# Attention products in single precision on pairs of 64x64 tiles instead of three half-precision products each

## The chip, the cores and the metric

One Trainium2 chip; the kernel runs on one of its eight cores. The metric is device time of one launch in microseconds (us), less is better. The kernel before takes 2324.98 us (median of 3 runs, 2323.55 to 2327.02).

## The reference, cut to what matters

Three stages follow each other on 4 x 768 = 3072 tokens: a linear attention with a delta rule (8 heads of 48), a mixture of 8 experts weighted by a Sinkhorn-normalized gate, and a gated two-layer network.

```python
def _attn_ref(q, k, v, beta):               # (4, 8, 768, 48)
    k_n = k / (np.linalg.norm(k, axis=-1, keepdims=True) + 1e-06)
    for t in range(S):
        y[:, :, t] = einsum('bhd,bhde->bhe', q[:, :, t], state)
        v_old = einsum('bhde,bhd->bhe', state, k_n[:, :, t])
        state = state + beta_t * outer(k_n[:, :, t], v_t - v_old)
def _moe_ref(x, w_gate, w1, w2):            # x (3072, 384), 8 experts, 1024 wide
    P = exp(x @ w_gate - max)
    for _ in range(8): normalize rows of P, then columns, times N / E
    for e in range(E): out += P[:, e:e+1] * (maximum(x @ w1[e], 0) @ w2[e])
def _moe2_ref(x, w1, w2, w3, w_out):
    return ((x @ w1) * (x @ w2) @ w3) @ w_out
```

## The kernel before

The attention is computed in 12 chunks of 64 tokens. The 32 heads (batch times head) lie as 16 groups of two: one head of a group on partitions 0 to 63, the other on 64 to 127. A matmul for both is a pair, one on the upper left 64x64 corner of the array and one on the lower right (`tile_position`). A chunk's work is done in two halves (hf) of 8 groups, so that a half's product fills one PSUM bank: 8 pairs.

Within a chunk the recurrence is solved with a triangular matrix T per head. The names that the rows below use:

- `gram`: k times k transposed, from `kt` (keys transposed). Its lower blocks go to `a0` (printed as `a`) and `g12` (printed as `g`).
- `invert(j)`: for the two chunks of pair j together, VectorE inverts 32x32 unit triangular blocks: a transposition into `asys` (L590), the product with beta (`bm`), recursive doubling with products and reductions, and two transpositions back (L650 into `asys`, L652 into `a0`). It is one long chain on DVE.
- `tt_make`: from the inverted blocks, two small fp32 products of 32x32 tiles (`xm` reads `asys` and `g12`; `om` reads `g12` and the staging tile `stg`), then T times beta as `tt`.
- `prep_q`: q and k give `pt`, masked.
- `seq(c)`, the chain over the chunks: `ks` (state times k, subtracted from `vs`, giving r), `um` (T times r gives u), `um2` (k times u added onto the state in PSUM, copied to s), `ym` (q times s plus pt times u, the output).

All these products except `xm` and `om` are made in half precision without losing single precision: every operand is split into a high and a low fp16 part, and `three` (L569) issues three matmul pairs for each. So each operand costs a copy to fp16 on ACT (the high part) and a subtraction on DVE or POOL (the low part), and the scales that keep the parts in range: k is divided by its norm and multiplied by 1024 before the split (`prep_k`), q by a power of two found from its largest sum of squares (`scale_chain`), v by one found in a first pass over all of v (`vscan`), T by 256. `kt` comes from PE transposes of the fp16 keys with an identity.

After a chunk its output goes to DRAM and back (`xs_d`, a change of layout), and the gate's logits (`lg`) and expert 0 (`e0`, fp32r matmuls of 128x128 by 256 columns, tiles `xr`, `wA`, `hA`) are computed for it; e0 of chunks 10 and 11 is left for later. When the logits of chunk 11 are there, the Sinkhorn iterations run and the remaining experts and the last network follow (phases B and C: 128x512 and 128x256 matmuls).

What sets the order: nothing is ordered by hand. `Plan.order` takes each operation with its engines, planned duration, priority and the buffers (`Ring`) it needs, and fixes an order for every engine. The constants of the plan (`PAIR`, the planned duration of one pair) only move instructions; the chip runs each engine's list in that order and waits where data or a buffer are late. Buffers that matter here: three for `kt` and k, one for v, two for `a0`, one for `asys`, `t`, `prod` and `g12`; attention has three PSUM banks at a time. SP issues nearly all transfers, in order.

Of the kernel before, what the change touches and what calls it, by code (L numbers as in the profile page):

```python
# [6 lines left out]
F32 = mybir.dt.float32  # L7
# [17 lines left out]
KS = 1024.0  # L25
TS = 256.0
KSL = 3
K16 = 3
NKR = 3
NA0 = 2  # L30
NSU = 2
NST = 2
NV = 1
# [4 lines left out]
NQ = 2  # L38
# [7 lines left out]
PAIR = .036  # L46
ZDVE = (0,)
ZPOOL = (1,)
# [240 lines left out]
def act(n, psum=False):  # L289
    return (n / 1.2 + (55 if psum else 95)) / 1000  # L290
# [14 lines left out]
class Kernel:  # L305
# [56 lines left out]
    def setup(self):  # L362
# [41 lines left out]
        id0 = lambda: T["a0"][:, NA0 - 1, 0:4].rearrange("p s c -> p (s c)")  # L404
        self.dma(id0, lambda: a["ident"], 65536, [], ["id0"], -10)
        for i in range(K16):
            dst = lambda i=i: T["k16"][:, i]
            prio = (-9, -8, 8, 8)[i]
            if i in ZDVE:
                g.op({"DVE": 2048 / 1900 + .07}, lambda e, dst=dst: nc.vector.memset(dst(), 0.0), w=[("kz", i)], prio=prio)  # L410
            elif i in ZPOOL:
                g.op({"POOL": 2048 / 1200 + .07}, lambda e, dst=dst: nc.gpsimd.memset(dst(), 0.0), w=[("kz", i)], prio=prio)
            else:
                self.dma(lambda dst=dst: dst().rearrange(FLAT), lambda: a["zeros"][:, 0:2048], 256 * 2048, [], [("kz", i)], prio)
        for nm in ("u16", "s16"):
# [6 lines left out]
        self.kring = Ring(range(KSL), fifo=True)  # L422
        self.k16ring = Ring(range(K16), fifo=True)
        self.sring = Ring(range(NSU), fifo=True)
        self.uring = Ring(range(NSU), fifo=True)
        self.stg = Ring(range(NST))
        self.kraw = Ring(range(NKR), fifo=True)
        self.tt16ring = Ring(range(NTC), fifo=True)
        self.qraw = Ring([0], fifo=True)
        self.vring = Ring(range(NV), fifo=True)  # L430
        self.qring = Ring(range(NQ), fifo=True)
        self.ptring = Ring(range(NPT), fifo=True)
# [7 lines left out]
        self.K, self.K16, self.S, self.Q, self.PT, self.TT, self.X, self.a0 = {}, {}, {}, {}, {}, {}, {}, {}  # L440
        self.SX = None


    def sc(self, i):
        return self.T["sml"][:, i:i + 1]

    def scale_chain(self, src, dst, inv, bits, prio, key):

        nc, g = self.nc, self.g
        s = self.psum.new("attn")  # L450
        c = self.sc
        g.op({"PE": .11}, lambda e: self.mm(self.ps(s, 1), self.T["ones"], c(src), start=True, stop=True),
             r=["ones", ("sml", src)], w=[s], prio=prio)

        def chain(e):
            nc.vector.tensor_scalar(out=c(src), in0=self.ps(s, 1), scalar1=1e-30, scalar2=None, op0=ALU.max)
        g.op({"DVE": .1}, chain, r=[s], w=[("sml", src)], prio=prio)
        g.op({"ACT": .15}, lambda e: nc.scalar.activation(out=c(src), in_=c(src), func=AF.Sqrt), r=[], w=[("sml", src)],
             prio=prio)

        def fin(e):
            nc.vector.tensor_scalar(out=c(src).bitcast(I32), in0=c(src).bitcast(I32), scalar1=0x7F800000, scalar2=None,
                                    op0=ALU.bitwise_and)
            nc.vector.tensor_scalar(out=c(inv), in0=c(src), scalar1=2.0 ** -bits, scalar2=None, op0=ALU.mult)
            nc.vector.reciprocal(out=c(dst), in_=c(inv))
        g.op({"DVE": .3}, fin, r=[], w=[("sml", src), ("sml", inv), ("sml", dst)], prio=prio)
# [4 lines left out]
    def vscan(self):  # L471

        nc, g, T = self.nc, self.g, self.T
        for i in range(NCH):
            s = (self.yring, self.vring)[i % 2].new()
            v = (lambda s=s: T["vs"][:, s.at].rearrange("p g d -> p (g d)")) if i % 2 else (
                lambda s=s: T["xst"][:, s.at].rearrange("p h f -> p (h f)")[:, 0:768])
            self.dma(v, lambda i=i: self.vsrc(i), 393216, [], [s], -3)
            g.op({"ACT": act(768) + .09}, lambda e, v=v, i=i: nc.scalar.activation(
                out=v(), in_=v(), func=AF.Square, accum_out=self.sc(41 + i)), w=[s, ("sml", 41 + i)], prio=VP)  # L480
        g.op({"DVE": .1}, lambda e: nc.vector.tensor_reduce(out=self.sc(12), in_=T["sml"][:, 41:41 + NCH], axis=AX.X, op=ALU.add),
             r=[("sml", i) for i in range(41, 41 + NCH)], w=[("sml", 12)], prio=-1)
        self.scale_chain(12, 13, 14, 10, -1, "v")


    def prep_k(self, c):
        nc, g, T = self.nc, self.g, self.T
        pr = 10.0 * (c // 2)
        pe = lambda d: d if c < 2 else {"POOL": d["POOL"]}
        kr = self.kraw.new()  # L490
        raw = [kr]
        kraw = lambda: T["kraw"][:, kr.at]
        self.dma(lambda: kraw().rearrange("p g d -> p (g d)"), lambda: self.a["k"][c], 393216, [], raw, pr - 20 + c % 2)
        pb = self.pring.new()
        sq = lambda: T["prod"][:, pb.at, 0:768].rearrange("p (g d) -> p g d", d=D)
        g.op(pe({"POOL": pool2(768), "DVE": dve(768)}), lambda e: self.tt(e, sq(), kraw(), kraw(), ALU.mult),
             r=raw, w=[pb, "sq"], prio=pr)
        nr = lambda i: T["nrm"][:, i]
        g.op({"DVE": dve(768)}, lambda e: nc.vector.tensor_reduce(out=nr(0), in_=sq(), axis=AX.X, op=ALU.add),
# [27 lines left out]
        if c % 2 == 0:  # L527
            self.a0[c // 2] = self.aring.new()
# [911 lines left out]
```

## Time and profile before

| | us |
|---|---|
| median of 3 runs | 2324.98 |
| profiled execution, its own time | 2326.66 |
| its span, first to last instruction | 2324.9 |
| PE busy in the span | 2191.2 (94%) |
| DVE busy | 1325.7 (57%) |
| ACT busy | 696.5 (30%) |
| POOL busy | 335.2 (14%) |
| mean granted TensorE clock | 0.959 |

The page is read by stage: the shares above are averages over the attention (about the first 550 us) and the experts and the last network after it, which have different limits. PE's busy time is modelled, so a busy PE need not be PE at its best: the granted clock beside it says which of its two levels it had. An fp32 matmul of the program shows as two MATMUL records with a weight load each; an fp16 one as one of each. Idle time of an engine is followed by what ended it.

### The profile page before, as it was taken

How to read it: one execution, taken by the hardware profiler on the slowest of the kernel's cores; microseconds unless marked ns; L12 is line 12 of the kernel's file. 1: busy time of each engine (PE TensorE's matmuls, PEld its weight loads, DVE VectorE, ACT ScalarE, POOL GpSimd, SP SyncE). 2: the span in 40 equal slices, each digit the busy share in tenths (PEclk: the TensorE clock that was granted, in tenths of full speed). 3: DMA queues.
4: the chain of work that ended last, by engine and by line, in shares of the span. 5: the costliest groups of instructions: out<-in, count | busy, mean ns of one | idle time of the engine just before them, and what ended most of it. 6: DMA issues, size and time to landing. Idle time of an engine off the chain costs nothing.

```text
span 2324.9 us, 47410 instructions
## 1 busy us (share of the span) xinstructions
PE 2191.2 (94%) x20519; PEld 1926.3 (83%) x20519; DVE 1325.7 (57%) x2312; ACT 696.5 (30%) x1398; POOL 335.2 (14%) x324
## 2 busy tenths in 40 slices
PE   2589999997799999999999999999999999999999
PEld 2488888887688888888888888888888888999999
DVE  8787787674877777777644444444444444322332
ACT  6446546544222223232211211111111111233332
POOL 5323334113211101111000000000000001300000
PEclk6697898898999999999999999999999999999999
DMA  6212112114533233232210101101010034500000
GB/s 196 64 52 76 53 52 63 51 41 125 169 94 111 94 95 116 87 118 90 79 46 14 46 14 46 41 19 46 14 46 28 19 122 104 109 15 21 15 15 21
DMA packets 135009, 152.60 MB, mean 66 GB/s; under 512 B 10640, under 2 KB 105168, under 8 KB 134032
## 3 DMA queue, kind: packets, MB, share of 16 engines
q1 hardware_dynamic: 115920, 127.82, 17.8%
q0 software_dynamic: 18880, 21.76, 3.7%
q8 instruction: 160, 2.62, 0.5%
q14 instruction: 49, 0.40, 0.1%
HBM read 118.24 MB, written 31.29 MB: 64 GB/s over the span
## 4 chain that ended last, share of the span: by engine, by line
PE 74%; DVE 2%; issue 1%; DMA 0%; ACT 0%; POOL 0%; SPq 0%; DVEq 0%; ACTq 0%; POOLq 0%
PE b L327 74%; DVE acc L338 1%; DVE p L341 0%; DVE p L338 0%; DMA xst<-xs_d 0%; DMA rawB<-in_moe_w 0%; DMA xs_d<-xst 0%; DVE cs L995 0%; DVE xT L338 0%; DVE rs L991 0%; DVE tmp L338 0%; DVE rs L992 0%; DVE cv L1205 0%; DVE hA L341 0%; DVE cv L341 0%
## 5 line engine op out<-in xcount | busy, mean ns | idle before, releaser
L327 PE MATMUL b<-xT,wA 128*128 128x512 f32 x2520 | 584.7, 389 | 0.0
L327 PEld LDWEIGHTS b<-xT,wA 128*128 128x128 f32 x2520 | 473.0, 188 | 98.2
L327 PE MATMUL b<-hA,wA 128*128 128x512 f32 (+1 forms) x2322 | 499.1, 356 | 3.9 <-DVE hA L341 3.1
L327 PEld LDWEIGHTS b<-hA,wA 128*128 128x128 f32 x2322 | 389.0, 191 | 65.9 <-DVE hA L341 4.8
L327 PE MATMUL b<-hB,wA 128*128 128x512 f32 (+1 forms) x1566 | 406.1, 387 | 0.0
L327 PEld LDWEIGHTS b<-hB,wA 128*128 128x128 f32 x1566 | 292.0, 189 | 58.9
L338 DVE TENSOR_TENSOR tmp<-b,pb 128x512 f32<-128x512 f32 x252 | 174.0, 691 | 241.3 <-PE b L327 240.7
L1108 ACT ACTIVATE hA<-b 128x512 fp32r<-128x512 f32 (+1 forms) x178 | 104.2, 585 | 649.9 <-PE b L327 639.8
L341 DVE SCALAR_TENSOR_TENSOR hA<-b,hA 128x512 fp32r<-128x512 f32 (+1 forms) x218 | 147.4, 677 | 178.4 <-ACT hA L1108 169.7
L327 PE MATMUL b<-xr,wA 128*128 128x256 f32 (+1 forms) x1368 | 238.7, 327 | 2.6 <-ACT wA L331 2.2
L327 PEld LDWEIGHTS b<-xr,wA 128*128 128x128 f32 x1368 | 204.6, 193 | 24.1 <-ACT wA L331 2.6
L327 PE MATMUL b<-xr,xT 128*128 128x256 f32 x1728 | 209.9, 283 | 0.0
L327 PEld LDWEIGHTS b<-xr,xT 128*128 128x128 f32 x1728 | 209.3, 192 | 0.0
L341 DVE SCALAR_TENSOR_TENSOR hB<-b,hB 128x512 fp32r<-128x512 f32 (+1 forms) x174 | 118.3, 681 | 152.2 <-ACT hB L1108 152.2
L338 DVE TENSOR_TENSOR acc<-acc,tmp 128x512 f32<-128x512 f32 x250 | 181.4, 726 | 6.5
L1108 ACT ACTIVATE hB<-b 128x512 fp32r<-128x512 f32 (+1 forms) x174 | 102.3, 588 | 196.4 <-PE b L327 196.4
L338 DVE TENSOR_TENSOR cv<-b,cv 128x256 f32<-128x256 f32 x96 | 40.7, 424 | 162.2 <-PE b L327 161.6
L338 POOL TENSOR_TENSOR wA<-rawB,wA 128x768 fp32r<-128x768 f32 x17 | 33.0, 1939 | 674.7 <-ACT wA L331 674.7
L338 POOL TENSOR_TENSOR cv<-cv 128x256 f32<-128x256 f32 (+1 forms) x68 | 52.6, 774 | 300.9 <-DVE cv L1205 174.6
L327 PEld LDWEIGHTS <-kt 64*64 64x64 f16 x3360 | 71.1, 123 | 21.3 <-issue 16.9
L331 ACT ACTIVATE cvs<-cv 128x256 fp32r<-128x256 f32 x72 | 28.9, 402 | 165.0 <-DVE cv L341 165.0
L331 ACT ACTIVATE wA<-rawB 128x768 fp32r<-128x768 f32 x56 | 45.9, 842 | 73.5 <-PE b L327 39.0
(174 smaller groups left out, 2222.4 us busy)
## 6 DMA issues: line engine op xcount, KB each, us to landing
pb<-p_d SPq DMA_DIRECT2D x90, 256.0 KB, 3.2
rawB<-in_moe_w SPq DMA_DIRECT2D x112, 192.0 KB, 3.3
w_d<-cvs SPq DMA_DIRECT2D x112, 128.0 KB, 2.0
cvr<-in_w3T SPq DMA_DIRECT2D x32, 256.0 KB, 2.6
xT<-w_d POOLq DMA_DIRECT2D x32, 256.0 KB, 3.5
vs<-in_v SPq DMA_DIRECT2D x18, 384.0 KB, 3.9
qraw<-in_qT SPq DMA_DIRECT2D x12, 512.0 KB, 4.2
cvr<-in_moe_w SPq DMA_DIRECT2D x24, 256.0 KB, 2.6
```

The costliest lines, as they stand in the source:

```text
L327: self.nc.tensor.matmul(*args, skip_group_check=True, **kw)
L331: self.nc.scalar.activation(out=out, in_=in_, func=AF.Copy, **({} if scale is None else {"scale": scale}))
L338: self.E[eng].tensor_tensor(out=out, in0=in0, in1=in1, op=op)
L341: self.nc.vector.scalar_tensor_tensor(out=out, in0=in0, scalar=scalar, in1=in1, op0=op0, op1=op1)
L1108: g.op({"ACT": act(N, True)}, lambda e, s=s, h=h, hx=hx, N=N: nc.scalar.activation(out=self.hv(h, hx, N)[:, 0], in_=self.ps(s, N), func=AF ...
```

## The change

The fp16 parts, the scales and the transposes go. Every attention product is issued as one fp32 matmul pair (`pair`) where `three` issued three fp16 pairs. k stays as it was loaded; its transposed form is loaded from DRAM (`kT`, laid out on the host). The norms of k are found for both chunks of a pair at once and folded in elsewhere: beta is divided by the norm twice, v is multiplied by the norm before T is applied. q and v are not scaled. The mask of `pt` is multiplied in by DVE straight from PSUM. The planned duration of a pair becomes .118; rings become four for k and kt, three for v and q. What follows `e0` (phases B and C) is not touched.

```diff
-PAIR = .036
+PAIR = .118
@@ prep_k
-        g.op(pe({"POOL": pool2(768), "DVE": dve(768)}), lambda e: self.tt(e, sq(), kraw(), kraw(), ALU.mult),
+        self.dma(lambda: T["kt"][:, k.at].rearrange("p g t -> p (g t)"), lambda: self.a["kT"][c], 524288, [], [k], pr - 20.1 + c % 2)
+        g.op({"ACT": act(768)}, lambda e: nc.scalar.activation(out=sq(), in_=T["kraw"][:, kr.at], func=AF.Square), r=[kr], w=[pb], prio=pr)
...
+                v.tensor_scalar(out=nv(), in0=nr(1), scalar1=0.5, scalar2=1e-6, op0=ALU.mult, op1=ALU.add)
+                v.reciprocal(out=nr(2), in_=nv())
+                v.tensor_tensor(out=bm(), in0=bm(), in1=nr(2), op=ALU.mult)
+                v.tensor_tensor(out=bm(), in0=bm(), in1=nr(2), op=ALU.mult)
...
-            for i in range(2):
-                def tr(e, i=i, hf=hf, s=s):
-                            self.mm(o[r, y], T["k16"][r, kc.at, hf, i, y], T["i128"][r, r], start=True, stop=True, tile_position=(64 * p, 64 * p))
-                     lambda e, i=i, hf=hf, s=s: self.copy(e, T["kt"][:, k.at, hf, i], self.ps(s, 8, 64)),
...
-                    self.three(lambda r: o[r, y], kt(0, y), kt(1, y), kt(0, y), kt(1, y))
+                    self.pair(lambda r: o[r, y], kt, kt, rows=D)
@@
-    def three(self, o, lh, ll, rh, rl, first=True, last=True):
-        for l, r, st, sp in ((lh, rh, first, False), (lh, rl, False, False), (ll, rh, False, last)):
-            for p in range(2):
-                rows = slice(64 * p, 64 * p + 64)
-                self.mm(o(rows), l(rows), r(rows), start=st, stop=sp, tile_position=(64 * p, 64 * p))
+    def pair(self, o, l, r, rows=64, cols=64, start=True, stop=True):
+        for p in range(2):
+            k = slice(64 * p, 64 * p + rows)
+            self.mm(o(slice(64 * p, 64 * p + cols)), l(k), r(k), start=start, stop=stop, tile_position=(64 * p, 64 * p))
@@ prep_q (the scaling, the split and the staging of q go)
+            g.op({"DVE": dve(512)}, lambda e, s=s, pt=pt, hf=hf: self.tt(
+                e, T["pt"][:, pt.at // 2, pt.at % 2], self.ps(s, 8, 64),
+                T["masks"][:, 0:64].rearrange("p (o t) -> p o t", o=1).to_broadcast([128, 8, 64]), ALU.mult), r=[s, "masks"], w=[pt], prio=pr)
@@ seq
-        g.op({"ACT": act(768) + .09}, lambda e: self.copy(e, va(), va(), self.sc(13)), r=[("sml", 13)], w=vk, prio=pr)
+        g.op({"POOL": 1.5, "DVE": dve(768) + .08}, lambda e: self.tt(
+            e, va(), va(), T["nv"][:, 16 * c:16 * c + 16].rearrange("p (s o) -> p s o", o=1).to_broadcast([128, NG, D]), ALU.mult),
+            r=[("nv", j)], w=vk, prio=10.0 * j + .5)
...
-            g.op({"ACT": act(384)}, lambda e, vv=vv, hf=hf: self.copy("ACT", T["r16"][:, 0, hf], vv()),
-            g.op({"DVE": dve(384), "POOL": pool2(384)}, lambda e, vv=vv, hf=hf: self.tt(
-                e, T["r16"][:, 1, hf], vv(), T["r16"][:, 0, hf], ALU.subtract),
...
-            g.op({"ACT": act(384, True)}, lambda e, s=s, hf=hf: self.copy(
-                "ACT", part("u16", u, hf, 0), self.ps(s, 8, D), 1.0 / TS), r=[s, "u16z"], w=uk[:1], prio=pr)
-            g.op({"DVE": dve(384)}, lambda e, s=s, hf=hf: self.stt(
-                part("u16", u, hf, 1), self.ps(s, 8, D), 1.0 / TS, part("u16", u, hf, 0), ALU.mult, ALU.subtract),
+            g.op({"ACT": act(384, True)}, lambda e, s=s, gs=gs: self.copy("ACT", T["u"][:, u.at, gs], self.ps(s, 8, D)),
+                 r=[s], w=[(u, hf)], prio=pr)
```

How the lists of DVE move, at two places in the fourth of the six rounds (pair 3). The number behind a name is the buffer; `b` is a PSUM bank, `a` is a0.

DVE right behind the inversion's last transposition, before:

```order
L652 STREAM_TRANSPOSE a_109<-t 128x32x32
L338 TENSOR_TENSOR stg<-a_109,bm 128x8x32
L338 TENSOR_TENSOR stg<-b_131,bm 32x8x32 x2
L338 TENSOR_TENSOR tt_94<-stg,tt_94 128x512
L338 TENSOR_TENSOR stg<-b_134,bm 32x8x32 x2
L341 SCALAR_TENSOR_TENSOR a_109<-b_128,masks,a_109 128x256
L338 TENSOR_TENSOR tt_94<-stg,tt_94 128x512
L338 TENSOR_TENSOR stg<-a_109,bm 128x8x32
L341 SCALAR_TENSOR_TENSOR a_109<-b_129,masks,a_109 128x256
L341 SCALAR_TENSOR_TENSOR u_98<-b_132,u_98 128x384
L341 SCALAR_TENSOR_TENSOR u_98<-b_133,u_98 128x384
```

The same place on DVE now:

```order
L561 STREAM_TRANSPOSE a_107<-t 128x32x32
L332 TENSOR_TENSOR tt<-a_107,bm 128x8x32 x3
L332 TENSOR_TENSOR tt<-b_131,bm 32x8x32 x2
L335 SCALAR_TENSOR_TENSOR a_107<-b_126,masks,a_107 128x256
L332 TENSOR_TENSOR tt<-b_129,bm 32x8x32 x2
L335 SCALAR_TENSOR_TENSOR vs<-b_127,vs 128x384
L332 TENSOR_TENSOR vs<-vs,nv 128x768
L335 SCALAR_TENSOR_TENSOR vs<-b_130,vs 128x384
```

The low parts of T (tt), u, and further down of s and r are gone from the list; tt is written directly, and the next chunk's v is multiplied by its norms in between.

DVE at the start of the next inversion (pair 4), before:

```order
L590 STREAM_TRANSPOSE asys<-a_109 128x1024
L592 STREAM_TRANSPOSE a_109<-bm 128x32
L338 TENSOR_TENSOR asys<-asys,a_109 128x1024
L338 TENSOR_TENSOR prod<-t,asys 128x4
L604 TENSOR_REDUCE t<-prod 128x4
L341 SCALAR_TENSOR_TENSOR hA<-b_129,hA 128x512
```

The same place on DVE now, from the sixth row behind the first transposition on:

```order
L446 TENSOR_SCALAR nv<-nrm 128x32
L447 RECIPROCAL nrm<-nv 128x32
L448 TENSOR_TENSOR bm<-bm,nrm 128x32
L449 TENSOR_TENSOR bm<-bm,nrm 128x32
L501 STREAM_TRANSPOSE a_107<-bm 128x32
L332 TENSOR_TENSOR vs<-vs,nv 128x768
L332 TENSOR_TENSOR asys<-asys,a_107 128x1024
L332 TENSOR_TENSOR pt<-b_125,masks 128x512
L332 TENSOR_TENSOR prod<-t,asys 128x4
L332 TENSOR_TENSOR pt<-b_131,masks 128x512
L513 TENSOR_REDUCE t<-prod 128x4
```

The norms, the product of v with them and four masks of pt (two are shown) now stand inside the inversion; the masks wait there for the products of q and k on PE, which PE's list has behind `ym` of the pair's second chunk and ahead of e0.

On PE one product (8 pairs) was 48 rows LDWEIGHTS and 48 rows MATMUL and is now one row, such as `L321 MATMUL b_127<-vs,tt 64x48 x16`. In each of the middle rounds PE's list has first xm and om, then the products of seq for two chunks with gram between them, then `ym` of the second chunk, the four products of `pt`, and 288 matmuls of e0; before, some of e0's stood among the attention products. From the logits of chunk 11 on, PE's list reads the same before and now to the end of the program.

## Rows read from the trace of the kernel before

**Rows 1.** The page: PE's busy tenths and its granted clock, 40 slices of 58 us.

```profile
PE   2589999997799999999999999999999999999999
...
PEclk6697898898999999999999999999999999999999
```

**Rows 2.** Busy time by stretch: us, PE, PEld, DVE, ACT, POOL (instructions), PEclk, DMA share, GB/s.

```profile
25.00:78.00 53.00, 8.02 (x222) 7.18 (x223) 51.28 (x73) 24.83 (x52) 30.36 (x21) 0.50 0.45 139
...
210.00:252.00 42.00, 41.26 (x729) 39.40 (x724) 40.56 (x54) 20.00 (x38) 20.34 (x15) 1.00 0.21 63
...
290.00:342.00 52.00, 47.65 (x810) 45.95 (x810) 46.43 (x65) 21.00 (x44) 17.73 (x15) 0.97 0.18 50
342.00:378.00 36.00, 31.39 (x1276) 29.00 (x1270) 18.75 (x42) 24.66 (x56) 6.27 (x7) 0.81 0.19 57
...
505.00:553.00 48.00, 38.52 (x1154) 35.70 (x1146) 15.99 (x37) 22.87 (x46) 9.38 (x8) 0.79 0.21 52
553.00:600.00 47.00, 35.78 (x231) 33.78 (x232) 36.80 (x76) 16.60 (x34) 15.59 (x14) 0.79 0.49 145
```

**Rows 3.** DVE's timeline, the transpositions that begin and end inversions: start, duration.

```profile
25.16 1.98 DVE L590 STREAM_TRANSPOSE asys<-a 128x1024 f32<-128x1024 f32 x1
...
117.44 1.97 DVE L590 STREAM_TRANSPOSE asys<-a 128x1024 f32<-128x1024 f32 x1
...
250.28 2.07 DVE L652 STREAM_TRANSPOSE a<-t 128x1024 f32<-128x1024 f32 x1
...
289.45 2.02 DVE L590 STREAM_TRANSPOSE asys<-a 128x1024 f32<-128x1024 f32 x1
...
462.39 1.95 DVE L590 STREAM_TRANSPOSE asys<-a 128x1024 f32<-128x1024 f32 x1
...
503.01 2.07 DVE L652 STREAM_TRANSPOSE a<-t 128x1024 f32<-128x1024 f32 x1
```

**Rows 4.** PE's timeline: start, duration with the last record's end, records.

```profile
76.45 3.46 PE L327 MATMUL b<-asys,g 32*32 32x32 f32 x122 [26.52 <-DVE asys L650]
...
406.23 4.48 PE L327 MATMUL b<-xr,wA 128*128 128x256 f32 x36
...
417.72 1.71 PE L327 MATMUL b<-asys,g 32*32 32x32 f32 x96
...
423.18 1.70 PE L327 MATMUL b<-kt 64*64 64x64 f16 x96
...
553.14 0.69 PE L327 MATMUL b<-xr,wg 128*16 128x256 f32 x3 [3.26 <-ACT xr L331]
```

**Rows 5.** Waits up to 650 us: total us, times, longest.

```profile
PEld L327 <- issue: 43.2, 57, 1.7
```

**Rows 6.** Groups of instructions up to 650 us, by shape: busy us, mean ns.

```profile
L338 POOL TENSOR_TENSOR stg<-stg,masks 128x512 f32<-128x512 f32 x24 | 34.1, 1428 | 8.5 <-ACT stg L331 8.3
...
L341 DVE SCALAR_TENSOR_TENSOR u<-b,u 128x384 f16<-128x384 f32 x24 | 13.3, 553 | 6.5 <-ACT u L331 6.2
...
L333 DVE CAST kt<-b 128x512 f16<-128x512 f32 x14 | 9.4, 684 | 6.1 <-PE b L327 6.1
```

**Rows 7.** DVE's timeline, four single instructions.

```profile
3.88 0.96 DVE L338 TENSOR_TENSOR prod<-kraw 128x768 f32<-128x768 f32 x1 [1.94 <-DMA kraw<-in_k]
...
112.24 1.58 DVE L338 TENSOR_TENSOR r<-vs,r 128x384 f16<-128x384 f32 x1
...
191.88 0.55 DVE L338 TENSOR_TENSOR r<-vs,r 128x384 f16<-128x384 f32 x1
...
256.06 0.17 DVE L509 TENSOR_TENSOR nrm<-nrm 128x16 f32<-128x16 f32 x1
```

**Rows 8.** A stretch of the first transfers, columns as rows 2.

```profile
4.00:8.00 4.00, 0.00 (x0) 0.00 (x0) 3.79 (x10) 0.90 (x2) 0.22 (x3) 1.00 1.01 333
```

**Rows 9.** DMA issues up to 60 us: KB, median us to landing.

```profile
masks<-in_masks SPq DMA_DIRECT2D x1, 37.5 KB, 5.4
```

**Rows 10.** The chain of work that ended last, from 500 us: start, duration.

```profile
544.34 0.70 ACT xst L331
```

More of the change, by code (lines that the diff above doesn't have):

```diff
@@ L37 @@
 NY = 1
-NQ = 2
 EB = 8
@@ L439, in setup @@
         self.hring = Ring(range(HA))
-        self.K, self.K16, self.S, self.Q, self.PT, self.TT, self.X, self.a0 = {}, {}, {}, {}, {}, {}, {}, {}
+        self.K, self.KR, self.S, self.Q, self.PT, self.TT, self.X, self.a0 = {}, {}, {}, {}, {}, {}, {}, {}
         self.SX = None
[L444 to L466, printed above, removed]
@@ L468, in vsrc @@
     def vsrc(self, c):
         return self.a["v"][c]
[L471 to L483, printed above, removed]
@@ L498, in prep_k @@
         nr = lambda i: T["nrm"][:, i]
-        g.op({"DVE": dve(768)}, lambda e: nc.vector.tensor_reduce(out=nr(0), in_=sq(), axis=AX.X, op=ALU.add),
-             r=[pb], w=["n0"], prio=pr)
-        g.op({"DVE": dve(16)}, lambda e: nc.vector.tensor_scalar(out=nr(0), in0=nr(0), scalar1=1e-30, scalar2=None,
-                                                                 op0=ALU.max), w=["n0"], prio=pr)
-        g.op({"ACT": .15}, lambda e: nc.scalar.activation(out=nr(1), in_=nr(0), func=AF.Sqrt), r=["n0"], w=["n1"], prio=pr)
@@ L516, in prep_k @@
-        kc = self.K16[c] = self.k16ring.new()
-        kz = [("kz", i) for i in range(K16) if i == c or c >= K16]
-        dst = lambda hf, i: T["k16"][:, kc.at, hf, i, :, 0:D]
-        for hf in range(2):
-            src = lambda hf=hf: kraw()[:, 8 * hf:8 * hf + 8]
-            g.op({"ACT": act(384)}, lambda e, src=src, hf=hf: self.copy("ACT", dst(hf, 0), src()),
-                 r=raw + kz, w=[(kc, "h", hf)], prio=pr)
-            g.op(pe({"POOL": .81, "DVE": dve(384)}), lambda e, src=src, hf=hf: self.tt(e, dst(hf, 1), src(), dst(hf, 0), ALU.subtract),
-                 r=raw + [(kc, "h", hf)], w=[(kc, "l", hf)], prio=pr)
@@ L834, in um2 @@
                     o = self.ps(s, 8, D)
-                    kv = lambda i, y: lambda r: T["k16"][r, kc.at, hf, i, y]
-                    uv = lambda i, y: lambda r: part("u16", u, hf, i)[r, y]
                     for y in range(8):
-                        self.three(lambda r: o[r, y], kv(0, y), kv(1, y), uv(0, y), uv(1, y), c == 0 and y == 0, True)
-                g.op({"PE": 24 * PAIR}, um2, r=uk + [(kc, j, hf) for j in "hl"], w=[s], prio=pr)
-                sk = [(nx, hf, 0), (nx, hf, 1)]
-                g.op({"ACT": act(384, True)}, lambda e, s=s, hf=hf: self.copy("ACT", part("s16", nx, hf, 0), self.ps(s, 8, D), 1.0 / KS),
-                     r=[s, "s16z"], w=sk[:1], prio=pr)
-                g.op({"DVE": dve(384)}, lambda e, s=s, hf=hf: self.stt(
-                    part("s16", nx, hf, 1), self.ps(s, 8, D), 1.0 / KS, part("s16", nx, hf, 0), ALU.mult, ALU.subtract),
-                    r=[s, sk[0], "s16z"], w=sk[1:], prio=pr)
+                        self.pair(lambda r: o[r, y], col("kraw", kr, 8 * hf + y), col("u", u, 8 * hf + y), cols=D,
+                                  start=c == 0 and y == 0, stop=True)
+                g.op({"PE": 8 * PAIR * .8}, um2, r=[(u, hf), kr], w=[s], prio=pr)
+                g.op({"ACT": act(384, True)}, lambda e, s=s, gs=gs: self.copy("ACT", T["st"][:, nx.at, gs], self.ps(s, 8, D)),
+                     r=[s], w=[(nx, hf)], prio=pr)
         for hf in range(2):
```

246 lines of the change are left out of this document (82 added, 164 removed).

## The prediction

> **What bounds the kernel now.** I read the page's slices first: from about 600 us on PE is busy in every slice at full clock [rows 1]. PE's list from the logits of chunk 11 on is the same before and now, and those logits start at 553.1 us [rows 4]. So I take the 1772 us behind them as fixed, the 47 us of the Sinkhorn part included, where PE is busy 35.8 of 47 [rows 2]: what the change is worth is by how much the logits of chunk 11 come earlier.
>
> Ahead of them the program is six rounds, one for each pair of chunks, and DVE's transpositions mark their parts [rows 3]. An inversion runs from L590 to the end of L652, and then a product stretch to the next L590. Round 0: inversion 25.2 to 78 (53; the stretch is in rows 2), product stretch to 117.4 (39), together 92.2. Rounds 1 to 4: 117.4 to 462.4, so 345.0, or 86.2 each; with an inversion of 42 where it is short (210 to 252, [rows 2]) and 52 where more of the attention's products stand beside it (290 to 342: PE busy 47.7). Product stretches are between 35.5 and 42.3, as 252.4 to 289.5 (37.1). The last inversion ends at 505.1, and 48.0 later come the logits. The stretches have different limits [rows 2]. In an inversion DVE is busy 40.6 of 42 us and PE, at full clock, has e0 beside it: both nearly full. In a product stretch DVE is busy about half (18.8 of 36) and PE 31.4, but at clock 0.81: some 38% of the time at 1.2 instead of 2.4 GHz, and with bubbles. There the chain counts: product, copy out of PSUM, low part, next product.
>
> **PE's work.** A record of 64 fp16 columns comes every 17.5 ns or so (1.70 us for 96), and one of 32 fp32 columns as well (1.71 for 96) [rows 4]; two corners work side by side, so a corner spends 35 on each. e0's 256 columns take 4.31/36 = 120 ns (to the next start at 410.5), little over a column per cycle of 2.4 GHz (107). If a column takes a cycle, 64 columns fill 13.3 of the 17.5 ns and 4.2 are left over; the fp32 record then streams its 32 columns twice. No row shows 64 fp32 columns. Bounds: 17.5 ns a record (nothing added) and 35 (double in everything). I take twice the streaming and the same 4.2: 30.9 ns, and 24.2 for 48 columns, nearest to the row of the same type. A product is 32 such records, so 0.99 us (0.77 for 48 columns; bounds 0.56 and 1.12) against 48 x 17.5 = 0.84 before. A round has 4 gram, 4 pt, 8 ym and 12 of ks, um and um2: before 28 x 0.84 + 8 transposes of 16 records (2.2) = 25.8; now 16 x 0.99 + 12 x 0.77 = 25.1. So PE's work stays as it was (bounds: 10 us less, 6 more a round); the gain must come from the waits.
>
> **What goes.** (1) Waits for issue: 43.2 us in 57 pieces, 7 a round, in the streams of short fp16 records [rows 5]. A product was 96 rows of PE's list and is 16 instructions, so I take them as gone (bounds 0 and 7). (2) The low parts: in the chain from um to um2 an ACT copy is followed by a DVE subtraction of 0.55 [rows 6], likewise for s, r and T, each with a handover; two chunks pass this chain in each round. (3) Most of POOL's work (masks of pt alone 34.1 us, [rows 6]). DVE instructions with two SBUF operands ran long beside it: the same r took 0.55 and 1.58 [rows 7].
>
> **The product stretch now.** Its work on PE: eight xm and om groups of 32 records, 4.5; 4 gram, 4.0; 12 of ks, um and um2, 9.2; ym of the first chunk, 4.0: 21.7 us at full clock. In front stand about 2 us until the first T is ready, behind the last gram two ACT copies and one DVE product, 1.5 with handovers; some of this overlaps, so 24. At the clock of before, 0.81, that is 24/0.81 = 29.6: I take 30, against 38.5 on average in rounds 1 to 4. All clocks warm would give 25.
>
> **The inversion now.** Start from a short one, 42.5. Added on DVE: the norms of both chunks, seven small ones of 0.17 to 0.25 with gaps (1.6); v times the norms, 0.96 by the row of the same shape; four masks of pt from PSUM, 0.68 each as the cast of the same shape (2.7). Gone: casts of kt, the q scales and part of v's updates (some 2.5), and waits for POOL (some 1.5). Sum 44. The masks stand early in the inversion and wait for PE, which has ym of the second chunk (4 us) and the four products (4) behind the last gram: at full clock the masks come about as late as DVE reaches them (6 us in), so I add nothing; behind them the whole inversion waits, and after it xm. On PE 288 matmuls of e0 (34.5) and those 8 with the logits need 45, so PE ends last by a little and I take 45. Round: 30 + 45 = 75; four rounds, 4 x (86.2 - 75) = 45.
>
> **Start.** The first inversion began at 25.2 behind norms, splits, transposes and gram. Now gram needs only kT, but the masks (for a0) stand tenth in SP's list, behind 4.2 MB. The first transfers ran at 333 GB/s [rows 8] and the masks landed 5.4 us after issue when less was ahead [rows 9]. 12.6 + 2 = 14.5, then four copies and the product: about 18.5. So 6.5 earlier. If the masks overtook, 12 earlier.
>
> **Round 0.** The inversion has no e0 beside it but expert 0's weights on POOL and ACT, as before, and a clock of 0.50 [rows 2]; without the k splits and the first pass over v I take 48 for 53, and the product stretch, cold at its start, 31 for 39: 13.
>
> **End.** Inversion 42.7 to 42. The 48.0 behind it hold a product stretch and, from the output's copy at 544.3 [rows 10] to the logits, 9 us of transfers that stay. No gram, no state for a next chunk, and no split of q late in it: 30 + 9 = 39. Together 10.
>
> **The sum.** 6.5 + 13 + 45 + 10 = 74.5 off the span of 2324.9: 2250. The profiled execution's own time was 1.7 above its span, and the median of the runs 1.7 below that time, so 2250 us is also the forecast for the median. Its own range is 2223 to 2278.
>
> **Rivals.** *Clock warm in the products.* Fewer bubbles could keep 2.4 GHz, as for 42 us beside e0 [rows 2]. Product stretch 25, inversion 44: round 69, four rounds 69; start and round 0 23, end 16: 108 off, 2217. For it: no waits for issue. Against: every product stretch before lost the clock, also where PE was busy.
>
> *Four passes at full price.* If each fp32 record costs twice an fp16 one in all it does, a product is 1.12. The product stretch's PE work grows by 20 x 1.12 - 13.2 - 4.0 = 5.2, to 29.2/0.81 = 36; ym and pt add 1 to the inversion: round 82, 4 x 4 = 17 off; start 6.5, round 0 5, end 4: 33 off, 2292. For it: the record of 32 columns carries the same 4.2 for half the width. The Trainium skill (FP8 and Floating Point Precision, section TensorE Precision Notes) says that true FP32 takes four passes through the array; against the three fp16 products of before that is a third more, 1.12 a product, and this rival's time. The trace shows two records, and it cannot tell whether a pass has its own 4.2.
>
> *Long inversions stay.* An inversion with ym and pt beside it took 52 before [rows 2], and now each has them. Round 82: 4 x 4 = 17; with start, round 0 and end 25: 42 off, 2283. Against: PE had more records there than now, and waits for issue among them.
>
> *Slower: the clock stays low.* If the fp32 stream runs at 1.2 GHz from the stretch's start: fp32 records then came every 26.8 ns ((79.72 - 76.45)/122, [rows 4]), 1.5 times, and wider ones nearer to 1.9. With 1.75 the stretch is 21.7 x 1.75 + 3.5 = 41.5, ym and pt take 14 instead of 8 and hold the masks, inversion 50: round 91.5, four rounds 21 lost; start 6.5 and round 0 0 gained, end 5 lost: 2345. It decides below a mean clock of about 0.59 in the product stretches (24/41, where a round reaches 86). For it: 0.79 to 0.81 before, though PE was busy. Against: the 0.81 held with more bubbles than now.
>
> **How the numbers follow.** Forecast 0.48, warm clock 0.19, four passes 0.16, long inversions 0.08, low clock 0.09. Predicted 2250. The range for 8 in 10 runs from the warm case to the dear ones, 2200 to 2297, leaving out the low clock and the far ends. A measurement tells about 0.2% (4.6 us) from no change. All cases but the last are faster: 0.88 with a little off for two misfortunes at once; same 0.04; slower 0.08.
>
> **What would show it.** Right: 64-column fp32 records at about 31 ns, nearly no waits for issue on PEld, transpositions L499 about 75 us apart and the first at 18.5, chunk 11's logits at about 479, and PE full from about 550 on. Wrong: records at 35 ns or more, clock below 0.7 between L561 and L499, DVE idle inside the inversion in front of the masks of pt, or a longer way from the logits to the end than 1772.

## The result and the profile after

The changed kernel takes 2262.7 us (median of 4 runs, 2260.68 to 2273.15) against 2326.0 for the kernel before on the same chip: ratio 0.974, 95% interval 0.971 to 0.977. The forecast was 2250 with a range of 2200 to 2297. The profiled execution took 2261.05, its span is 2259.3.

The page of the changed kernel, engines, PE's busy tenths and its granted clock in slices of 56 us:

```profile
PE 2173.7 (96%) x17133; PEld 1900.1 (84%) x17133; DVE 1229.3 (54%) x2152; ACT 569.4 (25%) x1147; POOL 173.6 (8%) x192
...
PE   2799999988999999999999999999999999999999
...
PEclk7899899999999999999999999999999999999999
```

They answer to [rows 1]: PE is full from the eleventh slice on, 565 us instead of 640, and ACT and POOL do less. DVE's transpositions after (L499 begins an inversion, L561 ends one; start, duration), as [rows 3]:

```profile
18.59 1.91 DVE L499 STREAM_TRANSPOSE asys<-a 128x1024 f32<-128x1024 f32 x1
...
99.61 1.96 DVE L499 STREAM_TRANSPOSE asys<-a 128x1024 f32<-128x1024 f32 x1
...
296.01 2.03 DVE L561 STREAM_TRANSPOSE a<-t 128x1024 f32<-128x1024 f32 x1
...
326.48 1.95 DVE L499 STREAM_TRANSPOSE asys<-a 128x1024 f32<-128x1024 f32 x1
...
398.13 1.96 DVE L499 STREAM_TRANSPOSE asys<-a 128x1024 f32<-128x1024 f32 x1
```

| | before | forecast | after |
|---|---|---|---|
| first inversion starts | 25.2 | 18.5 | 18.6 |
| round 0 | 92.2 | 79 | 81.0 |
| rounds 1 to 4, each | 86.2 | 75 | 74.6 |
| of it the product stretch | 38.5 | 30 | 30.0 |
| last inversion to the logits of chunk 11 | 90.7 | 81 | 81.0 |
| these logits start at | 553.1 | 479 | 479.1 |
| from there to the end | 1771.8 | 1772 | 1780.2 |

The logits come 74.1 us earlier, where 74.5 was forecast. Behind them, where the forecast had "fixed", 8.4 us are lost. The stretches after (us, PE, PEld, DVE, ACT, POOL, PEclk, DMA share, GB/s), as [rows 2]: an inversion, three product stretches, the last one with the transfers, and the Sinkhorn part:

```profile
218.10:252.20 34.10, 30.96 (x869) 29.05 (x863) 12.66 (x24) 15.33 (x34) 0.76 (x1) 0.80 0.39 115
...
252.20:296.00 43.80, 43.05 (x522) 41.83 (x517) 38.70 (x61) 9.44 (x21) 0.00 (x0) 1.00 0.17 53
...
298.00:326.50 28.50, 25.46 (x885) 23.90 (x879) 12.68 (x26) 15.39 (x34) 0.76 (x1) 1.00 0.45 138
...
370.90:398.10 27.20, 24.55 (x853) 23.10 (x848) 10.75 (x21) 13.78 (x32) 0.77 (x1) 1.00 0.28 81
...
441.00:479.00 38.00, 35.16 (x831) 32.85 (x824) 9.31 (x19) 14.04 (x32) 1.37 (x2) 0.96 0.27 70
...
479.00:526.00 47.00, 38.41 (x266) 35.50 (x266) 36.64 (x83) 18.51 (x38) 12.14 (x12) 0.93 0.61 186
```

The clock stands right of POOL. Of the stretches of rounds 0 to 4 three had 0.80 to 0.85 and took 30 to 34, as forecast from 0.81; the last two kept 1.00 and took 27 to 28, which is half of the way to the rival "clock warm". PE's timeline after, fp32 products (start, duration with the last record's end, records), as [rows 4]:

```profile
329.41 3.02 PE L321 MATMUL b<-qt,kt 48*64 48x64 f32 x96
332.36 0.63 PE L321 MATMUL b<-xr,wA 128*128 128x256 f32 x3
...
386.36 1.15 PE L321 MATMUL b<-kt 48*64 48x64 f32 x32
387.35 1.96 PE L321 MATMUL b<-vs,tt 64*64 64x48 f32 x61
```

(332.36 - 329.41)/96 is 30.7 ns a record, a gram 0.99 us: the forecast had 30.9 and 0.99. PE's waits for issue from the first product stretch to the logits (before from 78 to 553 us; after from 70 to 520 us, of which none lie behind the logits at 479):

```profile
PEld L327 <- issue: 39.7, 53, 1.6
```

```profile
PEld b L321 <- issue: 12.2, 20, 1.8
```

### The profile page after: what moved, and what is told of

It is laid out like the page before. It is cut to its first block, busy times and chain, and to the rows that moved or that the text cites. A ratio compares the mean times of both kernels' runs of the same rounds, so it can differ in the third digit from the quotient of the medians.

```text
span 2259.3 us, 40041 instructions
## 1 busy us (share of the span) xinstructions
PE 2173.7 (96%) x17133; PEld 1900.1 (84%) x17133; DVE 1229.3 (54%) x2152; ACT 569.4 (25%) x1147; POOL 173.6 (8%) x192
## 3 DMA queue, kind: packets, MB, share of 16 engines
q1 hardware_dynamic: 115632, 128.80, 18.6%
## 4 chain that ended last, share of the span: by engine, by line
PE 91%; DVE 4%; DMA 2%; ACT 2%; issue 1%; SPq 0%; POOL 0%; ACTq 0%; DVEq 0%
PE b L321 91%; DMA xst<-xs_d 1%; DVE prod L332 1%; DMA masks<-in_masks 0%; ACT g L325 0%; DMA kraw<-in_k 0%; DMA xs_d<-xst 0%; DVE t L525 0%; ACT tt L325 0%; SPq L352 0%; DVE pt L332 0%; DVE xs L525 0%; DVE p L332 0%; DVE xr L332 0%; ACT xr L325 0%
## 5 line engine op out<-in xcount | busy, mean ns | idle before, releaser
L321 PE MATMUL b<-xT,wA 128*128 128x512 f32 x2520 | 588.2, 390 | 0.0
L321 PEld LDWEIGHTS b<-xT,wA 128*128 128x128 f32 x2520 | 473.0, 188 | 102.4
L321 PE MATMUL b<-hA,wA 128*128 128x512 f32 (+1 forms) x2322 | 499.5, 356 | 0.0
L321 PEld LDWEIGHTS b<-hA,wA 128*128 128x128 f32 x2322 | 385.6, 190 | 68.4 <-DVE hA L335 0.4
L321 PE MATMUL b<-hB,wA 128*128 128x512 f32 (+1 forms) x1566 | 413.5, 391 | 0.0
L321 PEld LDWEIGHTS b<-hB,wA 128*128 128x128 f32 x1566 | 292.0, 189 | 64.4
L321 PE MATMUL b<-xr,wA 128*128 128x256 f32 (+1 forms) x1368 | 234.2, 325 | 2.6 <-ACT wA L325 2.2
L321 PEld LDWEIGHTS b<-xr,wA 128*128 128x128 f32 x1368 | 202.2, 191 | 24.8 <-ACT wA L325 2.6
L321 PE MATMUL b<-xr,xT 128*128 128x256 f32 x1728 | 209.9, 283 | 0.0
L321 PEld LDWEIGHTS b<-xr,xT 128*128 128x128 f32 x1728 | 209.3, 192 | 0.0
L321 PE MATMUL b<-asys,g 32*32 32x32 f32 x768 | 16.6, 204 | 49.0 <-DVE asys L559 48.8
```

The costliest lines, as they stand in the source:

```text
L321: self.nc.tensor.matmul(*args, skip_group_check=True, **kw)
```

## The experiments

Each time is compared with the kernel before on the same chip. Three theories stood at first: A, that moved addresses cost the 8.4 us; W, that waits for issue and the chain of low parts made the product stretch long; P, that it is PE's records.

**Addresses.** The new `nv` and `nrm` stand in the constants ahead of the experts' tiles, so `wA`, `hA`, `xr`, `xT` and `acc` lie 704 bytes a partition higher; `hB`, allocated from the other end, does not move.

```diff
-                  bm=((128, n), F32), nv=((128, n), F32), nrm=((128, 3, 32), F32),
+                  bm=((128, n), F32), pad=((128, 112), F32),
...
+                  nv=((128, n), F32), nrm=((128, 3, 32), F32))   # behind u
```

> The changed kernel with nv and nrm allocated behind u and 448 bytes of padding in their place: wg, wA, hA, xr, yr, xT and acc lie at the SBUF addresses that they have in the kernel before (704 bytes a partition lower than in the changed kernel); the order of every engine is the same. Theory A (the 8.4 us lost behind the logits of chunk 11 come with the shifted addresses): matmuls that read hA and hB with 512 columns come every 226.7 ns again instead of 231.5, logits to end 1772 us, time 2254. Rival (something else of the change, such as the different order of DVE and POOL at the start of phase B, or the run itself): still 231.5 ns, logits to end 1780, time 2262.

Measured: 2242.9 (5 runs), ratio 0.9635 [0.9616, 0.9654], 20 us less than the changed kernel; logits at 480.9, from there 1760.2. From the starts of their records, matmuls with 512 columns that read `hA`, `hB` and `xT` come every 226.7 ns, as in the kernel before; after they came every 231.6, 232.1 and 228.1 ns. The reverse in the kernel before:

```diff
-                  rs=((128, NTT), F32), cs=((128, NE), F32), sml=((128, 56), F32))
+                  rs=((128, NTT), F32), cs=((128, NE), F32), sml=((128, 56), F32),
+                  pad=((128, 176), F32))
```

> The kernel before with 704 bytes of padding in the constants, so that wg, wA, hA, xr, yr, xT and acc lie where the changed kernel has them; nothing else differs. Theory A (addresses): hA and hB matmuls go from 226.7 to about 231.5 ns, time 2326 + 8 = 2334. Rival (not the addresses): 226.7 ns and 2326.

Measured: ratio 1.0086 [1.0070, 1.0102], 2348.6 against 2327.6; logits to end 1790.9, so 19.2 more than before, with the 231.6, 232.1 and 228.1 ns of after. Theory A holds with more than twice its size: not 8 but 20 us. Three hundred us in which PE is full, of before, of e1, after, and of e2 (columns as above; PE's records in the first bracket):

```profile
1200.00:1500.00 300.00, 300.00 (x1325) 248.40 (x1324) 137.32 (x194) 54.24 (x88) 6.33 (x4) 1.00 0.12 36
```

```profile
1128.00:1428.00 300.00, 300.00 (x1325) 248.43 (x1324) 136.89 (x194) 52.21 (x84) 5.54 (x3) 1.00 0.11 33
```

```profile
1126.00:1426.00 300.00, 300.00 (x1307) 245.06 (x1307) 134.49 (x190) 52.80 (x85) 5.60 (x3) 1.00 0.11 34
```

```profile
1199.00:1499.00 300.00, 300.00 (x1307) 245.03 (x1306) 134.63 (x191) 52.30 (x84) 5.60 (x3) 1.00 0.10 32
```

Busy time and clock show nothing: all four say 300 of 300 at 1.00. Only the count tells: 1325 records or 1307, 226 or 230 ns each. Which tile is it?

```diff
-        self.open("wA", "left", wA=((128, EB, 1536), F32R))
+        self.open("wA", "left", wA=((128, EB, 1536), F32R), pad2=((128, 176), F32))   # on e1
```

> The addresses of before for the experts' weights wA alone: hA, xr, yr, xT and acc lie 704 bytes higher behind a piece of padding, as in the changed kernel; hB lies the same in all. Theory A1 (the place of the weights decides, since matmuls that read hB were slowed too and hB never moved): all 512-column matmuls at 226.7 ns, logits to end 1760. Rival A2 (the place of the tiles that stream past or of the sums, hA, xT, acc): 231 to 232 ns for hA and hB, logits to end about 1780.

2283.2 (one run; before 2331.4 there), logits to end 1797.6: A1 falls, but A2's numbers are not met either, since it is slower than both and the matmuls that read `xT` and `xr` are slow as well (`hA` and `xT` 233.4 ns, `hB` 231.2). Its 300 us:

```profile
1131.00:1431.00 300.00, 300.00 (x1291) 242.59 (x1290) 132.23 (x187) 52.26 (x84) 5.54 (x3) 1.00 0.10 32
```

So distances were the next theory:

```diff
-            self.open("hBp", "right", hB=((128, 5 - HA, 1024), F32R))
+            self.open("hBp", "right", hB=((128, 5 - HA, 1024), F32R), pad2=((128, 176), F32))   # on e1
```

> e1_addr_of_before with hB (and the tiles on its side: cv, cvr, cvs, pb, tmp) 704 bytes lower: wA, hA, xr, xT and acc keep the addresses of before, but hB now lies as far from wA (189760 bytes) as in the changed kernel. Theory A3 (the distance between the weights and the tile that streams past decides): the same numbers as in the changed kernel, 231.6 and 232.1 ns for hA and hB and 228.1 for xT, logits to end about 1780. Rival A4 (the places themselves decide, whatever the distance): other numbers, either 226.7 everywhere and 1760, or a third pattern.

2261.35 (one run), logits to end 1778.8, and spacings (from the starts of the records) of 231.7, 232.1 and 228.1 ns, those of the changed kernel to 0.1 ns, though `wA`, `hA` and `xT` lie where they lay before:

```profile
1128.00:1428.00 300.00, 300.00 (x1307) 245.08 (x1306) 134.16 (x191) 53.54 (x86) 5.56 (x3) 1.00 0.11 34
```

A3's numbers hold and A4 falls: not the places by themselves decide, but distances. The distance that A3 named cannot be the only one, though: `hA` and `xT` lie as far from `wA` in e9, and in the changed kernel, as in e1, and they are slowed all the same. What changed in both, against e1, is the distance between these tiles and those that are allocated from the other end, `hB` and its neighbours (`cv`, `pb`, `tmp`). Which pair of tiles it is was not tried, and e9 and e5 are one run each; their spacings are means over a thousand records and more.

**The low parts.** Behind r, u, s and T the old element-wise work, for u for instance:

```diff
+            g.op({"DVE": dve(384)}, lambda e, s=s, gs=gs: self.stt(
+                T["u"][:, u.at, gs], self.ps(s, 8, D), 0.0, T["u"][:, u.at, gs], ALU.mult, ALU.add), r=[s], w=[(u, hf)], prio=pr)
```

> The changed kernel with the element-wise work of the low parts back in the chain, and only that: behind the copies of u and s one DVE instruction of 128x384 from PSUM each, behind r and T an ACT copy and one DVE instruction (128x384 and 128x512), all of which leave the values as they are (0 times the operand is added). Products stay single fp32 pairs. Theory W (the product stretch is a chain, and the low parts were a good part of what was saved): per chunk r 0.45 + 0.55 + handovers 0.4, u and s 0.55 + 0.2 each, so some 2.9, for two chunks 5.8, T about 1; of that 4 to 6 a round comes through, 24 to 36 in all: 2287 to 2299. Rival P (the stretch is now bound by PE, busy 0.87 to 0.97 of it, and the two halves of a chunk hide each other's element-wise work): 0 to 8, so 2262 to 2270.

2260.2 (4 runs), ratio 0.9712 [0.9694, 0.9730]: nothing lost. An inversion and a product stretch of it:

```profile
91.50:139.80 48.30, 45.45 (x648) 43.98 (x644) 44.23 (x69) 14.02 (x29) 1.48 (x1) 1.00 0.22 66
...
293.70:319.00 25.30, 24.58 (x830) 23.60 (x825) 17.20 (x35) 16.47 (x39) 0.85 (x1) 1.00 0.42 124
```

The product stretches were even shorter (the clock was at 0.94 to 1.00 in rounds 1 to 4, PE busy 24.6 of 25.3), the inversions some 4 longer, since the plan puts more work there (648 records on PE in the one above, 364 to 522 in those after). Rounds 1 to 4 together took 298 us, as after. In the total P is right: the low parts came back for nothing. That they would cost nothing at the same clock is not shown, since after it was 0.80 and 0.85 in two of these four stretches, and the warmer clock may have paid for some of them.

**Three half-precision pairs again**, without splits:

```diff
+        half = lambda x: x.bitcast(BF16)[:, 1::2]
-            self.mm(o(slice(64 * p, 64 * p + cols)), l(k), r(k), start=start, stop=stop, tile_position=(64 * p, 64 * p))
+            self.mm(o(slice(64 * p, 64 * p + cols)), half(l(k)), half(r(k)), start=start, stop=False, tile_position=(64 * p, 64 * p))
+        for i in range(2):   # for both corners
+                self.mm(o(slice(64 * p, 64 * p + cols)), self.T["zz"][k, 0:cols], half(r(k)), start=False, stop=stop and i == 1, ...
```

> The changed kernel with each fp32 pair replaced by three half-precision pairs as before: the first multiplies the upper 16 bits of both operands (bfloat16), the second and third take a stationary tile of zeros, so the low parts' contribution is left out and the precision is lost; there is no split work. 96 weight loads and matmuls of half precision for a product instead of 64 fp32 records. Theory W (waits for issue in the streams of short half-precision records cost about 7 us a round): PE's work is 0.84 a product against 0.77 to 0.99, so neutral, and 5 to 7 a round is lost to waits PEld <- issue of some 35 to 43 us in all: 2290 to 2305. Rival P (those waits stood behind the split's late operands and are hidden otherwise): less than 12 us of issue waits more, 2258 to 2270.

2308.5 (4 runs), ratio 0.9906 [0.9884, 0.9928]; logits at 523.8, 44.7 later than after. Its waits from 70 to 520 us, and two product stretches:

```profile
PEld L322 <- issue: 47.3, 49, 3.2
```

```profile
153.00:189.00 36.00, 28.93 (x1176) 27.29 (x1173) 12.44 (x23) 14.29 (x32) 0.76 (x1) 0.64 0.33 99
...
319.00:355.00 36.00, 29.22 (x1247) 27.29 (x1241) 12.81 (x25) 15.26 (x34) 0.76 (x1) 0.72 0.38 110
```

Waits for issue rise by 47.3 - 12.2 = 35 us, and the clock falls to 0.64 to 0.78 in rounds 1 to 4. W holds here, 3.5 us beyond its range: 45 of the 74 us are lost again with the form of the instructions alone, DVE and ACT doing the same as after. How the 45 divide between waits and clock was not tried. The other 29 stay with what e4 also leaves out (splits, scales, transposes): against the kernel before, its first inversion starts 7.0 earlier, round 0 is 2.0 shorter, rounds 1 to 4 together 17.1, and the end 3.2.

**One half-precision pair**, to price PE's records (the first of those three lines, with `stop=stop`):

> The changed kernel with each fp32 pair replaced by one half-precision pair on the upper 16 bits of both operands; the low parts are left out and the precision is lost. A product is 0.28 us of PE instead of 0.77 to 0.99, everything else is the same. Theory P (after the change the product stretch is bound by PE's records): product stretches lose most of the 12 to 14 us that PE's work loses, 17 to 20 from an inversion's end to the next L500 instead of 30; with rounds of 62, chunk 11's logits at about 400, time 2185. Rival W (the stretch is bound by the chain of copies and waits, PE's work hides in it): stretches of 26 to 30, time 2245 to 2260.

2226.2 (4 runs), ratio 0.9562 [0.9541, 0.9583], logits at 446.4. Two product stretches:

```profile
138.00:163.40 25.40, 18.83 (x542) 16.05 (x534) 12.43 (x24) 13.89 (x31) 0.76 (x1) 0.53 0.44 139
...
278.00:304.80 26.80, 18.84 (x592) 15.93 (x587) 12.42 (x24) 14.76 (x34) 0.76 (x1) 0.62 0.47 147
```

The result lies between both theories: PE is busy 18 instead of 27 us in a stretch of rounds 1 to 4, and these shrink from 30 to 25 on average. With PE busy less the clock drops to 0.53 to 0.62, so what remains runs at little over 1.2 GHz. How much of the 25 is this clock and how much the chain of copies was not separated. In round 0 the rows of e4 and e10 print a clock of 0.99 and 1.00, but records of 32x32 come 26.5 ns apart there ((67.73 - 64.50)/122 in e10), the pace of the cold stretch in [rows 4] and not the 17.8 (1.71/96) of the warm one; so these two rows are no sign of a warm clock.

**Masks of pt on ACT and POOL** (on e1):

```diff
-            g.op({"DVE": dve(512)}, lambda e, s=s, pt=pt, hf=hf: self.tt(
-                e, T["pt"][:, pt.at // 2, pt.at % 2], self.ps(s, 8, 64),
+            g.op({"ACT": act(512, True)}, lambda e, s=s, pt=pt, hf=hf: self.copy("ACT", T["pt"][:, pt.at // 2, pt.at % 2], self.ps(s, 8, 64)),
+                 r=[s], w=[pt], prio=pr)
+            g.op({"POOL": pool2(512)}, lambda e, s=s, pt=pt, hf=hf: self.tt(
+                e, T["pt"][:, pt.at // 2, pt.at % 2], T["pt"][:, pt.at // 2, pt.at % 2],
```

> e1_addr_of_before with the masks of pt as before: ACT copies the product out of PSUM and POOL multiplies the mask in, instead of one DVE instruction from PSUM (four of 0.68 in every inversion). Theory D (POOL beside DVE costs DVE more than it takes off it): the inversions do not get shorter by 2.7, since 24 POOL instructions of 1.4 stretch DVE's two-operand instructions; time 2243 or up to 15 more. Rival (the inversion is bound by DVE, and 2.7 less is 2.7 less): six times 2.7 minus little, 2228 to 2232.

2235.3 (4 runs), ratio 0.9584 [0.9560, 0.9607], below e1's interval: by the ratios 12 us less, in the profiled executions 8.6 at the logits. On the same chip e6 and e7 below, which are e1 with little changed, have medians 7 to 9 us above this one. The masks by shape, first of the changed kernel, then of this one:

```profile
L332 DVE TENSOR_TENSOR pt<-b,masks 128x512 f32<-128x512 f32 x24 | 16.1, 682 | 1.0 <-PE b L321 0.8
```

```profile
L332 POOL TENSOR_TENSOR pt<-pt,masks 128x512 f32<-128x512 f32 x24 | 33.4, 1421 | 177.8 <-ACT pt L325 177.8
```

All six inversions together are 12 us shorter than in e1, product stretches 3 longer. The rival holds, nearly with its size: 33 us on POOL cost less than 16 on DVE, because DVE's chain sets the inversion.

**The start.** The masks' DMA first (priority -30 for -10), on e1:

> e1_addr_of_before with the DMA of the masks first in SP's list instead of tenth behind 4.2 MB. Theory (the masks set when a0 can be made): first inversion at 12 to 13 instead of 18.4, and the 6 us come through to the end: 2237. Rival (the gram waits for kT and k of both chunks as long, or bm and the norms are late next): start 16 to 18, time 2241 to 2243.

```profile
15.33 1.97 DVE L500 STREAM_TRANSPOSE asys<-a 128x1024 f32<-128x1024 f32 x1
```

The start is 3 us earlier, half of what the theory had, and the rival is nearer; the ratio, 0.9621 [0.9600, 0.9642], cannot be told from e1's.

**A warm clock in round 0**, on e1:

```diff
+            for i in range(21 if j == 0 else 0):   # two matmuls each, planned behind the first norms
+                        self.mm(self.bank[s.at].rearrange("p (o t) -> p o t", o=4), T["ones"], ..., start=True, stop=True)
```

> e1_addr_of_before with 42 fp32 matmuls of 128x128 by 512 columns of ones (their result isn't read) on PE in the first inversion, where it stands idle for 46 us. Theory C (round 0 is long because the clock is at 0.50 from 33.7 to 88.3): PE starts the first product stretch at full clock, the stretch takes 30 to 31 instead of 36.8 from the inversion's end to the next L500, 5 to 6 us sooner at the logits: 2237. Rival (the first stretch is long because the conversions of expert 0's weights and the loads crowd ACT and DVE): stretch 35 to 37, time 2243. If the clock doesn't hold to the end of the inversion, the same 2243 with 0.5 in the stretch's clock.

2242.65, ratio 0.9618 [0.9601, 0.9635]. PE's filling and the stretch behind:

```profile
19.51 34.60 PE L321 MATMUL b<-ones 128*128 128x512 f32 x80
```

```profile
64.80:102.40 37.60, 34.89 (x1040) 33.37 (x1042) 18.82 (x36) 18.60 (x40) 4.47 (x3) 0.80 0.40 114
```

It ended 11 us ahead of xm, and the stretch was as cold as without it (0.79 in e1). The last two runs put all together, without and with a filling to the inversion's end:

> A candidate to beat both: the changed kernel with the addresses of before (e1), the masks of pt on ACT and POOL (e8), the DMA of the masks first (e6), and v times the norms on POOL alone. If the three gains add, 20 + 9 + 3 and up to 0.9 for every chunk that DVE was given: 2225 to 2232. Rival (POOL's part is late then, and r with it): 2235 or more.

> e11_best with 48 fp32 matmuls of 128x128 by 512 columns of ones in the first inversion: in e7_fill 42 of them ended 11 us ahead of xm, and the clock was down again in the stretch behind; now they last to its end. Theory C (a cold clock makes round 0's product stretch long): clock above 0.9 in the first stretch and the first product at 1.0 us instead of 1.9, 4 to 6 us sooner than e11_best. Rival (ACT and DVE with the weights of expert 0): the clock is up, but the stretch stays at 36 and the time equals e11_best within 2 us.

e11: 2239.9, ratio 0.9614 [0.9592, 0.9636]; e12: 2237.2, ratio 0.9605 [0.9583, 0.9626]. Neither is told apart from the other, and neither beats e8: the gains did not add. The time of e11 is as its rival has it, but the rival's reason is not seen: no engine waits for POOL's product of v in either trace up to the logits. Why the gains did not add stays open. (e11's profiled execution took 2230.9, its other four 2239 to 2240.) In e12 the filling lasted to 59.1, 2.4 us ahead of xm, and yet:

```profile
17.63 41.47 PE L321 MATMUL b<-ones 128*128 128x512 f32 x96
...
61.53 3.18 PE L321 MATMUL b<-asys,g 32*32 32x32 f32 x128 [2.44 <-DVE asys L560]
65.28 1.46 PE L321 MATMUL b<-tt,g 32*32 32x32 f32 x32 [0.56 <-ACT g L325]
66.66 1.97 PE L321 MATMUL b<-kt 48*64 48x64 f32 x32
```

```profile
63.00:97.60 34.60, 32.45 (x961) 30.86 (x957) 14.79 (x33) 19.68 (x42) 8.33 (x5) 0.81 0.46 135
```

In the 2.4 us without work the clock is still 1.00. From 61.5 to 65.3, with xm, it is 0.59, and behind that 0.50, so the gram takes 1.8 us instead of 0.99. Theory C was not put to the test, since its condition, a warm first stretch, was never reached. The lowest median is e8's, 2235 against 2263 for the changed kernel; its interval overlaps with those of e11 and e12.

## Why the prediction was right, and where it was not

- *PE's work neutral, 30.9 ns a record, 0.99 a product*: right, 30.7 and 0.99. The rival "four passes at full price" falls by this. The Trainium skill (FP8 and Floating Point Precision, section TensorE Precision Notes) counts four passes for true FP32. The trace agrees so far: two corners side by side with two records each make 4 x 30.7 = 123 ns for a pair, which has room for four passes of 64 columns (107 at 2.4 GHz), but not for four passes at the price of whole half-precision records (4 x 35 = 140). The 107 is an estimate at one column a cycle, and 16 ns are left beside it. Products of 48 columns took 0.72 to 0.93 us where 0.77 was forecast.
- *Waits for issue gone*: right in the main, but not gone. 53 pieces became 20, and 12.2 of 39.7 us stayed. The form of the instructions, waits and clock together, is the largest part of the gain: e4 takes 45 of the 74 us back.
- *The low parts shorten the chain*: wrong in the total, since e3 puts them back for nothing. The forecast of 30 for the stretch did not rest on their price but on PE's 21.7 and the waits beside it, 24 at full clock, over 0.81. That 30.0 was measured is luck: the two stretches at full clock took 27 to 28 and not 24, and the clock of the four was 0.91 on average. With this clock the same sum gives 26.
- *Less POOL beside DVE*: wrong for the masks, which are cheaper on POOL (e8); the 2.7 us that the forecast added for them in an inversion need not have been paid. Where it did show was a place that the forecast had called fixed: the Sinkhorn loop. DVE there, before and after:

```profile
564.11 2.59 DVE L338 TENSOR_TENSOR xT<-acc,xT 128x768 fp32r<-128x768 f32 x1
...
566.85 2.70 DVE L341 SCALAR_TENSOR_TENSOR p<-p,cs 128x192 f32<-128x192 f32 x1
```

```profile
488.91 0.95 DVE L332 TENSOR_TENSOR xT<-acc,xT 128x768 fp32r<-128x768 f32 x1
...
490.01 0.36 DVE L335 SCALAR_TENSOR_TENSOR p<-p,cs 128x192 f32<-128x192 f32 x1
```

- *"I take the 1772 us behind them as fixed"*: this is the step that failed, and the prediction's own sign for it, a longer way from the logits to the end, is there. PE's list is the same, but it is not the only thing that sets the time. Two shifts of opposite sign lie behind the 8.4 us, and that so little was missing is luck. The moved tiles cost 1780.2 - 1760.2 (e1) = 20.0. The rest, 1760.2 - 1771.8 = -11.6, is gained almost wholly within 100 us of the logits, 8.7 of it by the last product of `cs` in the Sinkhorn loop (594.84 - 553.14 = 41.7 before, 512.08 - 479.08 = 33.0 after). In the kernel before, POOL subtracts beside the two DVE instructions above, which are 4 us longer than after:

```profile
564.04 1.84 POOL L338 TENSOR_TENSOR xT<-acc,xT 128x768 fp32r<-128x768 f32 x1 [6.18 <-ACT xT L331]
...
567.51 1.81 POOL L338 TENSOR_TENSOR xT<-acc,xT 128x768 fp32r<-128x768 f32 x1
```

PE waits for them, before and after:

```profile
571.29 0.60 PE L327 MATMUL b<-cs,ones 128*128 128x8 f32 x2 [4.01 <-DVE cs L995]
```

```profile
492.90 0.39 PE L321 MATMUL b<-cs,ones 128*128 128x8 f32 x2 [0.82 <-DVE cs L850]
```

Behind the wait of 4.01 the granted clock is 0.50 (571.3 to 576.3), and PE's way to the next product of `cs` takes 5.1 us; after it is 1.00 there and takes 2.9. PE's waits for `cs` in all (11.7 before, 6.8 after in these 47 us) are the lateness of DVE seen from PE and no gain of their own. All this is read from the traces and was not tried by itself.

- *Round 0, start and end*: within 2 us. That the masks set the start was half right (e6: 3 us).
- *Clock*: taken at 0.81, it was 0.80 to 0.85 in three product stretches and 1.00 in two; why in these was not settled. In the forecast it was a rival of its own, but in rounds 1 to 4 it goes with the form of the instructions: 0.64 to 0.78 in e4 and 0.53 to 0.62 in e10.

## What to carry to other kernels

A stage whose instruction list does not change is not fixed: look at where its tiles will lie and at what the other engines do beside it, and compare records in a stretch in which PE is full, since busy time and clock do not show a matmul that takes 2% longer. An operation that feeds a half-busy chain may cost nothing while another engine is full; put it back by itself before it is counted as a gain. Many short instructions cost twice in this kernel, by waits for issue and by the lower clock that came with them (e4), so fewer and longer ones won at about equal work.

## What the runs showed of the hardware

704 bytes a partition more or less between the tiles of a full stage move PE from 1325 to 1307 or 1291 records in 300 us at granted clock 1.00, 20 and 37 us of 1760. Matmuls of 256 columns on 128x128 kept their 120 ns (from the starts of the records) in all six kernels of that group. PE's timeline of e5, where `hB` is not touched:

```profile
1206.74 1.56 PE L321 MATMUL b<-xT,wA 128*128 128x512 f32 x6
1208.14 2.27 PE L321 MATMUL b<-xr,wA 128*128 128x512 f32 x9
```

Six records take 1.40 us, 233 ns each, against 226 in the kernel before (300/1325). The Trainium skill (TensorE: Matmul & The Clock Gate, section Step-by-step: what each phase is for) says that weights and the streaming operand are read through ports of their own, so that loading the next weights takes nothing from the running matmul. Between e1 and e5 these tiles moved against `wA` and against `hB` by 704 bytes, and the records became 3% longer. So the page's sentence does not cover all that tiles in SBUF can do to a matmul; whether the loading of weights has a part in it, and by which mechanism the records grow, stays open.
